# Joined load of k and q, earlier output weights, and weight conversion on GpSimd in an attention and gated-MLP kernel

## The chip, the core and the metric

The kernel runs on one NeuronCore of a Trainium2 chip. The metric is the device time of one execution in microseconds (us), taken as the median of several executions of the same program. Five engines work side by side, each through its own queue in order: TensorE (PE, matmuls; PEld are its weight loads), VectorE (DVE), ScalarE (ACT), GpSimd (POOL) and SyncE (SP), which here issues every DMA.

## What is computed

For 8 batches of 8 heads, 576 positions and head dimension 64, the kernel does causal attention with a bias made of prefix sums, and puts the result through a gated MLP with a spatial mixing step.

```python
scores = scale * np.matmul(q, k.transpose(0, 1, 3, 2))
cum = np.cumsum(np.maximum(s, 0.0), axis=-1)
bias = -(cum[:, :, :, None] - cum[:, :, None, :])
scores = np.where(causal, -1000000000.0, scores + np.minimum(bias, 0.0))
attn = softmax(scores)
x = np.matmul(attn, v)                       # (B, S, 512) after joining heads
h = np.maximum(x @ w_in, 0.0)                # d_ff 1024
u, v = h[..., :512], h[..., 512:]
v_n = (v - mu) / np.sqrt(var + 1e-06)
v_s = np.einsum('ts,bsd->btd', w_spatial, v_n) + b_spatial[None, :, None]
out = (u * v_s) @ w_out
```

q, k, v and s are float32, and the MLP's weights w_in, w_spatial and w_out come as they are drawn: w_in and w_out are 64-bit floats.

## The kernel before

Matmuls run in 16 bits. Every float32 operand is split into a high part (its float16 rounding) and a low part (the rest, in float16), and a product is three matmuls: high by high, high by low, low by high.

**Heads in pairs.** The 64 heads are 32 pairs, four pairs to a batch. For a pair, `load_raw` fetches k and q as float32 tiles with the head dimension in the partitions, both into partitions 64 to 127 and again into 0 to 63 (four loads for pairs 3 to 5; three for later pairs, where the second load of q is left out). `split_raw` makes four float16 tiles, each one of three that rotate: KA and QA hold the high parts in partitions 64 to 127 (and constants and prefix sums in the lower ones, `aux_rows`), KB and QB hold low and high parts stacked, so that one matmul over 128 partitions adds both cross products. k goes through VectorE (L251 rounds, L255 subtracts), q through ScalarE (L259) and GpSimd (L239, four pieces of 288 columns). For pairs below 6 the copies of the high parts to the other half of the partitions are ScalarE steps (L249, L261); for later pairs they are DMAs from SBUF to SBUF (L257, L263). Pairs 0 to 2 multiply the float32 tiles directly (L310). The raw tiles of k and q have one buffer each.

**Attention.** `s_pass` makes a pair's scores (L316) in PSUM, masks and takes the minimum (VectorE, L320), takes the exponential (ScalarE, L326), normalises into high and low parts (L335, L336), and transposes the result by DMA (L341). `av_pass` multiplies by V (L414, L421) and evacuates the result to xt: high part on ScalarE (L427), low part on VectorE (L428). The bank of av has one buffer.

**MLP.** `mlp` runs by batch: the gate half (L455) with its normalisation (L471 to L489), the other half (L505), the spatial product (L518 to L521) with the gating (L523 to L526), and the output product (L540), evacuated at L543 and stored at L545.

**Weights.** The 64-bit weights are fetched as integers (`fetch_w64`), and `split_w64` makes float32 of them by bit operations on VectorE (L167, L168, L170), zeroes what is too small (ScalarE squares at L173, VectorE compares and multiplies at L174), and hands the float32 tile to `split_w`: high part on ScalarE (L148); low part on VectorE (L150), or by a scaling on ScalarE (L152) and a subtraction on GpSimd (L153). The constants `N_W1`, `N_W2`, `N_W3` and `N_W4` are 2, 1, 5 and 0: two tiles of w_in's gate half, one of its other half and all five of w_spatial take VectorE; three and two tiles of w_in and the four of w_out take GpSimd. `load_wout` fetches and converts one of four tiles of w_out, all through the one buffer of the tag "wst", which also holds one tile of w_in before and the bias rows.

**Order.** Every step is put into a list with a position (`at`, `units`); the list is sorted by position and emitted in that order. TensorE runs exactly in the order of emission. On the other engines a scheduler that simulates the program orders instructions, with what is emitted earlier ahead of what is emitted later. Up to position 12.416 (`G_END`) most steps are also kept behind the last step that is marked as first on their engine. Pair p's scores lie at positions 2p to 2p + 5/3, its av at 2p + 3.72 (pair 3: 9.4), and batch b's MLP at 8b + 10.3 to 8b + 18; the output product of batch 0 begins at 16.1. The load of pair p lies at 2p - 5.2, its split at 2p - 1.2. `load_wsp` lies at 11 to 12.2, `load_wtail` at 13.

Of the kernel before, what the change touches and what calls it, by code (L numbers as in the profile page):

```python
# [7 lines left out]
F16 = mybir.dt.float16  # L8
# [10 lines left out]
SW = 64.0  # L19
# [10 lines left out]
@with_exitstack  # L30
def attn_gated_mlp(ctx, tc, qT, kT, v, s, w_in, w_spT, b_sp, w_out, outT):
    nc = tc.nc
    P = 128
    NHB, D, H, S = qT.shape
    B, H = NHB // 2, 2 * H
    NPAIR = H // 2
# [76 lines left out]
    def native_tiles(pair):  # L113


        hs = slice(2 * (pair % 2), 2 * (pair % 2) + 2)
        tags = (("g1", "g2"), ("xt1", "xt2"), ("xt1", "xt2"), ("rawk", "rawq"))[pair]
        raw_tiles(pair // 2, hs, tags, (1, 2, 2, N_RB)[pair])
        first_ins["c"] = [raw_rows(pair // 2, hs, nm, 1) for nm in "kq"][1].ins

# [26 lines left out]
    def split_w(dst1, dst2, raw, sc, dve):  # L147
        nc.scalar.activation(dst1, raw, AF.Copy, bias=0.0, scale=sc)  # L148
        if dve:
            nc.vector.scalar_tensor_tensor(out=dst2, in0=raw, scalar=sc, in1=dst1, op0=ALU.mult, op1=ALU.subtract)  # L150
            return
        nc.scalar.activation(raw, raw, AF.Copy, bias=0.0, scale=sc)  # L152
        nc.gpsimd.tensor_tensor(out=dst2, in0=raw, in1=dst1, op=ALU.subtract)  # L153

# [5 lines left out]

    def split_w64(dst1, dst2, st, tag_t, dve):

# [10 lines left out]
        nc.scalar.activation(sq, sq, AF.Square, bias=0.0, scale=1.0)  # L173
        nc.vector.scalar_tensor_tensor(out=tf, in0=sq, scalar=2.0 ** -30, in1=tf, op0=ALU.is_ge, op1=ALU.mult)  # L174
        split_w(dst1, dst2, tf, SW, dve)

# [6 lines left out]
    def load_win(hf, c):  # L183
        split_w64(win1[:, c, hf * NF:(hf + 1) * NF], win2[:, c, hf * NF:(hf + 1) * NF], wsts.pop((hf, c)),
                  "hv" if hf else "ob", c < (N_W1 if hf else N_W2))

    def load_wout(c):
        split_w64(wo1[:, c], wo2[:, c], fetch_w64(w_out[c * P:c * P + P], "wst"), "ob", c < N_W4)

    def load_wsp(c):  # L190
        st = wk.tile([P, S], F32, tag="ob", bufs=2, name="wsp_st")
        nc.sync.dma_start(out=st, in_=w_spT[c * P:c * P + P])
        split_w(ws1[:, c], ws2[:, c], st, SWSP, c < N_W3)

    def load_wtail():
        s4 = wk.tile([P, S], F32, tag="ob", bufs=2, name="wsx_st")
        nc.sync.dma_start(out=s4[0:TAIL], in_=w_spT[NFULL * P:S])
        nc.sync.dma_start(out=s4[TAIL:2 * TAIL], in_=w_spT[NFULL * P:S])
        split_w(wx1, wx2, s4, SWSP, N_W3 > 4)
        bf = wk.tile([1, S], F32, tag="ob", bufs=2, name="bf")  # L200
# [16 lines left out]

    def raw_tiles(hb, hs, tags=("rawk", "rawq"), bufs=1):

        for tag, nm in zip(tags, "kq"):  # L220
            raws[hb, hs.start, nm] = wk.tile([P, hs.stop - hs.start, S], F32, tag=tag, bufs=bufs, name=f"{nm}raw{hb}")

    def raw_rows(hb, hs, nm, top):
        rows = slice(64 * top, 64 * top + 64)
        if nm == "k" or top or 2 * hb + hs.start // 2 < N_CD:
            return nc.sync.dma_start(out=raws[hb, hs.start, nm][rows], in_=(kT if nm == "k" else qT)[hb, :, hs])

    def load_raw(hb, pr):
        hs = slice(2 * pr, 2 * pr + 2)
        raw_tiles(hb, hs, bufs=N_RB)  # L230
        for top in (1, 0):
            for nm in "kq":
                raw_rows(hb, hs, nm, top)

    def pieces(eng, out, in0, in1):
        for j in range(2):
            for hf in range(2):
                c = slice(hf * TH, hf * TH + TH)
                eng.tensor_tensor(out=out[:, j, c], in0=in0[:, j, c], in1=in1[:, j, c], op=ALU.subtract)  # L239

    def split_raw(hb, nm, pr):

        p = 2 * hb + pr
        i = p % 3
        raw = raws[hb, 2 * pr, nm]
        lo, hi = slice(0, 64), slice(64, 128)
        if nm == "k":
            if p < N_CD:
                nc.scalar.copy(KA[i][hi], raw[hi])  # L249
            if p < N_KA:  # L250
                nc.vector.tensor_copy(KB[i], raw)  # L251
            else:
                nc.scalar.copy(KB[i], raw)
            eng = nc.gpsimd if p < N_KP else nc.vector
            eng.tensor_tensor(out=KB[i][lo], in0=raw[lo], in1=KB[i][lo], op=ALU.subtract)  # L255
            if p >= N_CD:
                nc.sync.dma_start(out=KA[i][hi], in_=KB[i][hi])  # L257
        else:
            (nc.scalar.copy if p < N_QA else nc.vector.tensor_copy)(QA[i][hi], raw[hi])  # L259
            if p < N_CD:  # L260
                (nc.scalar.copy if p < N_QA else nc.vector.tensor_copy)(QB[i][lo], raw[lo])  # L261
            else:
                nc.sync.dma_start(out=QB[i][lo], in_=QA[i][hi])  # L263
            pieces(nc.gpsimd, QB[i][hi], raw[hi], QA[i][hi])

# [125 lines left out]
    def av_pass(pair):  # L391
# [40 lines left out]
    def mlp(b):  # L432
# [32 lines left out]
        for t in range(NC5):  # L465
# [13 lines left out]
            nc.vector.bn_aggr(out=mv, in_=st if tail else st[:, 0])  # L479
            nc.gpsimd.tensor_scalar(rs, mv[:, 1:2], 1.0e-6, None, op0=ALU.add)  # L480
            nc.gpsimd.tensor_tensor(out=rs, in0=rs, in1=mhalf, op=ALU.pow)
# [4 lines left out]
            else:  # L486
                d1, d2 = vn1[:, t], vn2[:, t]
            nc.scalar.activation(d1, hv, AF.Copy, bias=0.0, scale=SVN)
            nc.vector.scalar_tensor_tensor(out=d2, in0=hv, scalar=SVN, in1=d1, op0=ALU.mult, op1=ALU.subtract)  # L489
            if tail:  # L490
# [91 lines left out]
    at(-18.9, True, native_cum, 1)  # L582
    at(0.5, True, behind, "c", load_raw, 1, 1)
    at(0.6, True, init_static, 0)
# [12 lines left out]
    for hb in range(2, NHB):  # L597
        for pr in range(2):
            p = 2 * hb + pr
            at(2 * p - 5.2, False, load_raw, hb, pr)  # L600
            at(2 * p - 1.2, False, aux_rows, p)
            for nm in "kq":
                at(2 * p - 1.2, False, split_raw, hb, nm, pr)
        at(4 * hb - 0.5, False, fetch_v, hb)
        at(4 * hb + 1.5, False, load_v, hb)
    for c in range(KC):
# [4 lines left out]
        at(11 + 0.4 * c, False, load_wsp, c)  # L611
        at(13.5 + 0.5 * c, False, load_wout, c)
    at(13, False, load_wtail)
    for p in range(NP):
        units([2 * p + k / 3 for k in range(6)], p < 4, s_pass, p)
        at_av = 2 * p + 3.72 if p != 3 else 9.4
        units([at_av], p < 4, av_pass, p)
    for b in range(B):
# [61 lines left out]
```

## Time and profile before

| | |
|---|---|
| three runs | 740.40, 741.07, 741.52 us |
| median | 741.07 us |
| profiled execution | 741.57 us |
| its span in the trace | 739.8 us |
| mean granted clock of TensorE | 0.928 |
| DMA traffic | 119.09 MB, 161 GB/s |
| HBM read, written | 46.71 MB, 9.44 MB |

The span is what the trace covers of the profiled execution; 1.8 us lie around it. In the rows of the profile, "L414" is line 414 of the kernel, a name such as `xt<-av` is what is written and read, "x32" a count, and an arrow in brackets names the time an engine stood idle before the instruction and what ended that idle time. In a row of the waits the numbers are the total in us, how often, and the longest. In a row of the timeline the first number is the start in us and the second the length. A group of instructions has, behind its count, busy us, mean ns of one, and the idle time before.

### The profile page before, as it was taken

The numbers are of one execution on the slowest core, as the hardware profiler recorded it, in microseconds if no ns is written. First come the engines' busy times: TensorE is split into PE (matmuls) and PEld (weight loads), VectorE is DVE, ScalarE is ACT, GpSimd is POOL, SyncE is SP. The second block draws the span as 40 slices with busy tenths as digits, with TensorE's granted clock in tenths as the row PEclk, the third lists the DMA queues.
The fourth block names the chain that finished last, engine by engine and source line by source line (L and its number), as shares of the span: only waits on it lengthen the run. The fifth ranks groups of instructions, "written<-read, shape, count | busy, mean of one in ns | idle before, by whom it ended". The sixth has DMA issues, their size and how long they took to land. (4 is left out here: it accounts for less than half of the span.)

```text
span 739.8 us, 15952 instructions
## 1 busy us (share of the span) xinstructions
PE 609.2 (82%) x5696; PEld 420.0 (57%) x5696; DVE 607.5 (82%) x1660; ACT 528.2 (71%) x1334; POOL 175.8 (24%) x226
## 2 busy tenths in 40 slices
PE   4555454576659899999899899899998998999998
PEld 2243222255436677667665667477756774677676
DVE  8968699969839999889988997899979997985431
ACT  5957677567638788879786978778787887875422
POOL 7002335303302322142213321132223222100100
PEclk9777677599759999999999999999999999999999
DMA  9798776948638779987998799969997798465001
GB/s 203 177 223 166 187 179 155 205 110 195 159 85 190 150 152 189 208 193 127 202 209 196 139 202 187 216 132 193 190 216 145 180 184 161 76 126 121 33 13 64
DMA packets 243261, 119.09 MB, mean 161 GB/s; under 512 B 213887, under 2 KB 227373, under 8 KB 243182
## 3 DMA queue, kind: packets, MB, share of 16 engines
q1 hardware_dynamic: 243182, 118.08, 75.1%
q8 instruction: 44, 0.72, 0.4%
q14 instruction: 35, 0.29, 0.1%
HBM read 46.71 MB, written 9.44 MB: 76 GB/s over the span
## 5 line engine op out<-in xcount | busy, mean ns | idle before, releaser
L239 POOL TENSOR_TENSOR QB<-qraw,QA 64x288 f16<-64x288 f32 x116 | 123.4, 1095 | 296.5 <-ACT QA L259 219.8
L320 DVE CUSTOM_DVE_ANT_0 psS<-psS,mb 128x512 f32<-128x512 f32 (+2 forms) x320 | 155.0, 495 | 14.9 <-PE psS L316 13.9
L326 ACT ACTIVATE p<-psS,mx 128x256 f32<-128x256 f32 (+3 forms) x256 | 132.9, 523 | 48.0 <-DVE mx L320 44.2
L336 DVE SCALAR_TENSOR_TENSOR pb<-p,sm,pb 128x384 f16<-128x384 f32 (+3 forms) x256 | 129.7, 548 | 0.5 <-ACT pb L335 0.3
L335 ACT ACTIVATE pb<-p,sm 128x384 f16<-128x384 f32 (+3 forms) x256 | 122.7, 556 | 9.1 <-ACT p L326 5.1
L540 PE MATMUL ops<-g,wo 128*128 128x288 f16 x768 | 105.3, 291 | 16.7 <-ACT wo L148 12.0
L316 PE MATMUL psS<-KA,QA 128*128 128x128 f16 (+1 forms) x348 | 82.2, 310 | 44.3 <-ACT p L326 32.8
L505 PE MATMUL ups<-xt,win 128*128 128x288 f16 x768 | 105.1, 290 | 15.7 <-ACT win L148 6.0
L518 PE MATMUL sps<-ws,vn 128*128 128x288 f16 x768 | 105.7, 288 | 11.0 <-DVE g L523 11.0
L455 PE MATMUL vps<-win,xt 128*128 128x512 f16 (+1 forms) x576 | 106.1, 356 | 10.5 <-ACT ob L543 8.5
L505 PEld LDWEIGHTS <-win 128*128 128x128 f16 x768 | 74.7, 99 | 45.0 <-issue 12.4
L540 PEld LDWEIGHTS <-wo 128*128 128x128 f16 x768 | 75.4, 99 | 42.9 <-ACT wo L148 12.6
L518 PEld LDWEIGHTS <-vn 128*128 128x128 f16 x768 | 74.3, 98 | 36.4 <-issue 14.1
L316 PE MATMUL psS<-KB,QB 128*128 128x128 f16 (+1 forms) x348 | 88.9, 306 | 0.0
L455 PEld LDWEIGHTS <-xt 128*128 128x128 f16 (+1 forms) x576 | 48.9, 104 | 60.3 <-issue 22.1
L414 PE MATMUL av<-pT,V 128*64 128x128 f16 (+2 forms) x960 | 67.8, 295 | 13.8 <-DMA pT<-pb 13.8
L414 PEld LDWEIGHTS <-V 128*64 128x64 f16 x960 | 55.1, 119 | 31.6 <-issue 20.0
L316 PEld LDWEIGHTS <-QA 128*128 128x128 f16 x348 | 30.3, 102 | 45.4 <-issue 37.7
L480 POOL TENSOR_SCALAR rs<-mv 128x1 f32<-128x1 f32 x40 | 10.3, 257 | 190.3 <-DVE mv L479 173.7
L326 ACT ACTIVATION_READ_ACCUMULATOR p<-psS,mx 128x1 f32 x256 | 50.6, 198 | 0.0
L543 ACT ACTIVATE ob<-ops 128x288 f32<-128x288 f32 x64 | 25.0, 413 | 30.9 <-PE ops L540 17.4
L316 PEld LDWEIGHTS <-QB 128*128 128x128 f16 x348 | 29.9, 103 | 26.5 <-issue 19.7
(117 smaller groups left out, 890.3 us busy)
## 6 DMA issues: line engine op xcount, KB each, us to landing
kraw<-in_kT_dram SPq DMA_DIRECT2D x61, 288.0 KB
qraw<-in_qT_dram SPq DMA_DIRECT2D x35, 288.0 KB
out_dram<-ob SPq DMA_DIRECT2D x32, 288.0 KB
vraw<-in_v_dram SPq DMA_DIRECT2D x16, 512.0 KB
wst<-in_w_in_dram SPq DMA_DIRECT2D x8, 512.0 KB
QB<-QA SPq DMA_DIRECT2D x26, 144.0 KB
KA<-KB SPq DMA_DIRECT2D x26, 144.0 KB
vraw<-in_v_dram SPq DMA_DIRECT2D x16, 128.0 KB
```

Source lines behind the costliest of these rows:

```text
L239: eng.tensor_tensor(out=out[:, j, c], in0=in0[:, j, c], in1=in1[:, j, c], op=ALU.subtract)
L316: nc.tensor.matmul(ps[m, c0:c0 + w], U[i][:, g, q0:q0 + n], T[i][:, g, k0:k0 + w], start=st, stop=not st)
L320: nc.vector.tensor_tensor_reduce(out=ps[:, c0:c0 + w], in0=ps[:, c0:c0 + w], in1=mask, op0=ALU.add, op1=ALU.min, scale=-0.125, scalar=3.0e ...
L326: nc.scalar.activation(p32, ps[:, c0:c0 + w], AF.Exp, bias=mx[:, col:col + 1], scale=-1.0, accum_out=sm[:, acc:acc + 1])
L335: nc.scalar.activation(dst[:, off:off + w], p32, AF.Copy, bias=0.0, scale=sm[:, col:col + 1])
L336: nc.vector.scalar_tensor_tensor(out=dst[:, n + off:n + off + w], in0=p32, scalar=sm[:, col:col + 1], in1=dst[:, off:off + w], op0=ALU.mul ...
L414: nc.tensor.matmul(dst, V[i][:, jc, h + j], rhs, start=jc == n == 0 and q0 > 0, stop=jc == 3 and n == 2)
L455: nc.tensor.matmul(ps[m, 0:w], xx[:, c, t * P:t * P + (m.stop - m.start)], ww[:, c, NF + g * w:NF + g * w + w], start=c == n == 0, stop=c ...
L505: nc.tensor.matmul(ps[:, 0:TH], ww[:, c, fs], xx[:, c, ts], start=n == 0, stop=n == 3 * KC - 1)
L518: nc.tensor.matmul(ps[:, 0:TH], vv[:, c, fs], ww[:, c, ts], start=n == 0, stop=False)
L540: nc.tensor.matmul(ps[:, 0:TH], ww[:, f, ms], gg[:, f, ts], start=n == 0, stop=n == 3 * FC - 1)
L543: nc.scalar.activation(ob[:, ts], ps[:, 0:TH], AF.Copy, bias=0.0, scale=1.0 / (SG * SW))
```

## The change

One input, kqT, holds k's and q's transposed rows one above the other, so that a pair's k and q come by one load of 128 partitions: k in the lower 64, q in the upper. The raw tile has two buffers. VectorE rounds k into a tile kh in the lower partitions, two DMAs copy that into KA and KB, and a third copies QA's high part into QB; this holds for all pairs from 3 on. `split_w64` now compares and scales on GpSimd, multiplies on GpSimd in two halves, and subtracts there in two halves, for all twelve tiles. The low parts of w_spatial are subtracted on GpSimd too, in two halves, after a scaling on ScalarE. The evacuation of av becomes a unit of its own, 0.35 positions behind its matmuls. The factor 64 of the normalised gate goes into the reciprocal root. `load_wout` of tile c moves from position 13.5 + 0.5 c to 10.6 + 1.1 c.

```diff
@@ split_w
         nc.scalar.activation(raw, raw, AF.Copy, bias=0.0, scale=sc)
-        nc.gpsimd.tensor_tensor(out=dst2, in0=raw, in1=dst1, op=ALU.subtract)
+        h = raw.shape[1] // 2
+        for c in (slice(0, h), slice(h, 2 * h)):
+            nc.gpsimd.tensor_tensor(out=dst2[:, c], in0=raw[:, c], in1=dst1[:, c], op=ALU.subtract)
@@ split_w64
         nc.scalar.activation(sq, sq, AF.Square, bias=0.0, scale=1.0)
-        nc.vector.scalar_tensor_tensor(out=tf, in0=sq, scalar=2.0 ** -30, in1=tf, op0=ALU.is_ge, op1=ALU.mult)
-        split_w(dst1, dst2, tf, SW, dve)
+        nc.gpsimd.tensor_scalar(sq, sq, 2.0 ** -30, SW, op0=ALU.is_ge, op1=ALU.mult)
+        h = n // 2
+        for c in (slice(0, h), slice(h, n)):
+            nc.gpsimd.tensor_tensor(out=tf[:, c], in0=sq[:, c], in1=tf[:, c], op=ALU.mult)
+        nc.scalar.copy(dst1, tf)
+        for c in (slice(0, h), slice(h, n)):
+            nc.gpsimd.tensor_tensor(out=dst2[:, c], in0=tf[:, c], in1=dst1[:, c], op=ALU.subtract)
@@ load_wsp, load_wtail
-        split_w(ws1[:, c], ws2[:, c], st, SWSP, c < N_W3)
+        split_w(ws1[:, c], ws2[:, c], st, SWSP, False)
...
-        split_w(wx1, wx2, s4, SWSP, N_W3 > 4)
+        split_w(wx1, wx2, s4, SWSP, False)
@@ load_raw, split_raw
+    def load_raw(p):
+
+        hb, pr = divmod(p, 2)
+        raws[p] = wk.tile([P, 2, S], F32, tag="raw", bufs=2, name=f"raw{p}")
+        nc.sync.dma_start(out=raws[p], in_=kqT[hb, :, 2 * pr:2 * pr + 2])
...
         if nm == "k":
...
+            kh = wk.tile([64, 2, S], F16, tag="kh", bufs=1, name=f"kh{p}")
+            nc.vector.tensor_copy(kh, raw[lo])
+            nc.sync.dma_start(out=KA[i][hi], in_=kh)
+            nc.sync.dma_start(out=KB[i][hi], in_=kh)
+            nc.vector.tensor_tensor(out=KB[i][lo], in0=raw[lo], in1=kh, op=ALU.subtract)
         else:
...
+            nc.scalar.copy(QA[i][hi], raw[hi])
+            nc.sync.dma_start(out=QB[i][lo], in_=QA[i][hi])
+            for j in range(2):
+                for c in (slice(0, TH), slice(TH, S)):
+                    nc.gpsimd.tensor_tensor(out=QB[i][hi, j, c], in0=raw[hi, j, c], in1=QA[i][hi, j, c],
+                                            op=ALU.subtract)
@@ av_pass
+        yield
         both = [(av, x1[:, pr, 0:512], x2[:, pr, 0:512])]
@@ mlp
-            nc.gpsimd.tensor_scalar(rs, mv[:, 1:2], 1.0e-6, None, op0=ALU.add)
+
+            nc.gpsimd.tensor_scalar(rs, mv[:, 1:2], 1.0e-6, 1.0 / (SVN * SVN), op0=ALU.add, op1=ALU.mult)
...
-            nc.scalar.activation(d1, hv, AF.Copy, bias=0.0, scale=SVN)
-            nc.vector.scalar_tensor_tensor(out=d2, in0=hv, scalar=SVN, in1=d1, op0=ALU.mult, op1=ALU.subtract)
+            nc.scalar.copy(d1, hv)
+            nc.vector.tensor_tensor(out=d2, in0=hv, in1=d1, op=ALU.subtract)
@@ the plan
-        at(13.5 + 0.5 * c, False, load_wout, c)
+        at(10.6 + 1.1 * c, False, load_wout, c)
...
-        units([at_av], p < 4, av_pass, p)
+        units([at_av, at_av + 0.35], p < 4, av_pass, p)
@@ kernel
-        'qT': inputs['q'].reshape(2 * B, H // 2, S, D).transpose(0, 3, 1, 2),
-        'kT': inputs['k'].reshape(2 * B, H // 2, S, D).transpose(0, 3, 1, 2),
+        'kqT': _np.concatenate([inputs[n].reshape(2 * B, H // 2, S, D).transpose(0, 3, 1, 2) for n in 'kq'], axis=1),
```

More of the change, by code (lines that the diff above doesn't have):

```diff
@@ L30, in attn_gated_mlp @@
 @with_exitstack
-def attn_gated_mlp(ctx, tc, qT, kT, v, s, w_in, w_spT, b_sp, w_out, outT):
+def attn_gated_mlp(ctx, tc, kqT, v, s, w_in, w_spT, b_sp, w_out, outT):
     nc = tc.nc
     P = 128
-    NHB, D, H, S = qT.shape
-    B, H = NHB // 2, 2 * H
+    NHB, D, H, S = kqT.shape
+    B, H, D = NHB // 2, 2 * H, D // 2
     NPAIR = H // 2
@@ L116, in native_tiles @@
         hs = slice(2 * (pair % 2), 2 * (pair % 2) + 2)
-        tags = (("g1", "g2"), ("xt1", "xt2"), ("xt1", "xt2"), ("rawk", "rawq"))[pair]
-        raw_tiles(pair // 2, hs, tags, (1, 2, 2, N_RB)[pair])
-        first_ins["c"] = [raw_rows(pair // 2, hs, nm, 1) for nm in "kq"][1].ins
+        tags = ((("g1", 1), ("g2", 1)), (("xt1", 2), ("xt2", 2)), (("xt1", 2), ("xt2", 2)))[pair]
+        raw_tiles(pair // 2, hs, tags)
+        first_ins["c"] = [raw_rows(pair // 2, hs, nm) for nm in "kq"][1].ins
     def native_sel(pair):
@@ L159, in fetch_w64, with split_w64 @@
         return st
-    def split_w64(dst1, dst2, st, tag_t, dve):
+    def split_w64(dst1, dst2, st, tag_t):
         n = st.shape[1]
@@ L184, in load_win @@
         split_w64(win1[:, c, hf * NF:(hf + 1) * NF], win2[:, c, hf * NF:(hf + 1) * NF], wsts.pop((hf, c)),
-                  "hv" if hf else "ob", c < (N_W1 if hf else N_W2))
+                  "hv" if hf else "ob")
     def load_wout(c):
-        split_w64(wo1[:, c], wo2[:, c], fetch_w64(w_out[c * P:c * P + P], "wst"), "ob", c < N_W4)
+        split_w64(wo1[:, c], wo2[:, c], fetch_w64(w_out[c * P:c * P + P], "wst"), "ob")
     def load_wsp(c):
@@ L216, in attn_gated_mlp @@
     raws = {}
[L218 to L243, printed above, removed]
+    def raw_tiles(hb, hs, tags):
+        for (tag, bufs), nm in zip(tags, "kq"):
+            raws[hb, hs.start, nm] = wk.tile([P, 2, S], F32, tag=tag, bufs=bufs, name=f"{nm}raw{hb}")
+    def raw_rows(hb, hs, nm):
+        src = kqT[hb, 0:64, hs] if nm == "k" else kqT[hb, 64:128, hs]
+        return nc.sync.dma_start(out=raws[hb, hs.start, nm][64:128], in_=src)
@@ L244, in split_raw @@
+    def load_raw(p):
+        hb, pr = divmod(p, 2)
+        raws[p] = wk.tile([P, 2, S], F32, tag="raw", bufs=2, name=f"raw{p}")
+        nc.sync.dma_start(out=raws[p], in_=kqT[hb, :, 2 * pr:2 * pr + 2])
+    def split_raw(nm, p):
         i = p % 3
-        raw = raws[hb, 2 * pr, nm]
+        raw = raws[p] if nm == "k" else raws.pop(p)
         lo, hi = slice(0, 64), slice(64, 128)
         if nm == "k":
[L248 to L257, printed above, removed]
-        else:
[L259 to L264, printed above, removed]
@@ L582, in attn_gated_mlp @@
     at(-18.9, True, native_cum, 1)
-    at(0.5, True, behind, "c", load_raw, 1, 1)
+    at(0.5, True, behind, "c", load_raw, 3)
     at(0.6, True, init_static, 0)
@@ L588, in attn_gated_mlp @@
     for nm in "kq":
-        at(2.1, True, split_raw, 1, nm, 1)
+        at(2.1, True, split_raw, nm, 3)
     at(2.1, True, native_tiles, 2)
@@ L599, in attn_gated_mlp @@
             p = 2 * hb + pr
-            at(2 * p - 5.2, False, load_raw, hb, pr)
+            at(2 * p - 5.2, False, load_raw, p)
             at(2 * p - 1.2, False, aux_rows, p)
             for nm in "kq":
-                at(2 * p - 1.2, False, split_raw, hb, nm, pr)
+                at(2 * p - 1.2, False, split_raw, nm, p)
         at(4 * hb - 0.5, False, fetch_v, hb)
```

## The prediction

> **What bounds the kernel now.** I read the busy totals first, then busy time by stage, then what TensorE waited for in each stage, then the timelines around its longest waits.
>
> ```profile
> PE 609.2 (82%) x5696; PEld 420.0 (57%) x5696; DVE 607.5 (82%) x1660; ACT 528.2 (71%) x1334; POOL 175.8 (24%) x226
> ```
>
> TensorE and VectorE are equally busy over the whole, which hides two stages. The rows below give start:end, length, then busy time (and count) of PE, PEld, DVE, ACT, POOL, then granted clock, DMA share and GB/s.
>
> ```profile
> 0.00:213.24 213.24, 114.47 (x908) 71.38 (x909) 176.89 (x439) 142.46 (x332) 62.24 (x72) 0.78 0.77 174
> 213.24:672.00 458.76, 430.69 (x4254) 301.59 (x4253) 408.42 (x1172) 362.78 (x950) 109.29 (x144) 0.99 0.83 171
> ```
>
> From 213 us on PE is busy 430.69 of 458.76 us at clock 0.99: it is the bound, and 28 us is all that better order could give there. Before 213 it is idle 213.24 - 114.47 = 98.8 us. VectorE works 177 of those 213 us, so it is the busiest, but it also has pauses. What PE waited for, first in that stage, then (last row) after it:
>
> ```profile
> PE psS L316 <- ACT p L326: 30.4, 6, 9.7
> PE av L414 <- DMA pT<-pb: 13.0, 3, 7.4
> PE ops L540 <- ACT wo L148: 12.0, 2, 7.8
> PE psS L316 <- DMA KA<-cc: 9.6, 1, 9.6
> ...
> PE ops L540 <- POOL wo L153: 3.8, 2, 2.5
> ...
> PE vps L455 <- ACT ob L543: 8.5, 5, 2.4
> ```
>
> So the change must be priced in the first 213 us. What it saves there moves the start of the saturated stage and reaches the end nearly whole. The steady stage I leave unpriced, at 0, with 8 us (the size of its largest wait) either way for a changed order.
>
> **The change, part by part.** The base is the profiled execution, 741.57 us (span 739.8 and 1.8 around it); the runs' median is 741.07, 0.5 lower.
>
> *A. The evacuation of av is emitted 0.35 positions later.*
>
> ```profile
> 53.96 3.15 PE L414 MATMUL av<-pT,V 128*64 128x384 f16 x27 [7.44 <-DMA pT<-pb]
> ...
> 57.36 0.60 ACT L427 ACTIVATE xt<-av 128x512 f16<-128x512 f32 x1 [7.67 <-PE av L414]
> ...
> 58.19 0.69 ACT L326 ACTIVATE q<-psS,mx 128x512 f32<-128x512 f32 x1
> ...
> 58.86 1.92 ACT L335 ACTIVATE pb<-p,sm 128x384 f16<-128x384 f32 x4
> ```
>
> PE waits 7.44 us for the transposed weights; ScalarE has the evacuation at the head of its queue and stands 7.67 us behind it, though the softmax work of 0.69 and 1.92 us behind it needs no av. Emitted later, that work should go first: at least 2.6 us, at most the 7.67. I take 2.6, since little more was ready. Later on the evacuation also comes later; cost 0, hidden by the one-pair distance to the next av, and if that cover fails, see the third rival.
>
> *B. Joined load, copies by DMA.*
>
> ```profile
> kraw<-in_kT_dram SPq DMA_DIRECT2D x61, 288.0 KB
> qraw<-in_qT_dram SPq DMA_DIRECT2D x35, 288.0 KB
> ...
> QB<-QA SPq DMA_DIRECT2D x26, 144.0 KB
> KA<-KB SPq DMA_DIRECT2D x26, 144.0 KB
> ```
>
> Three pairs stay as 6 loads of 288 KB; 29 pairs take one load of 576 KB and three copies of 144 KB. That is 1,728 + 16,704 + 12,528 = 30,960 KB in place of 96 x 288 + 52 x 144 = 35,136: 4.2 MB less. For pairs 3 to 5 four loads become one: 576 KB less each, 3.3 us at the stage's 174 GB/s. In SP's queue a pair goes from five issues to four (pairs 3 to 5: four both ways). The new wait is that KA, KB and the low half of QB hang on DMAs behind SP's queue, where transposes, aux rows and loads are queued; for pairs 3 to 5 ScalarE wrote them directly. In exchange ScalarE is freed of these:
>
> ```profile
> 67.02 1.15 ACT L249 CAST KA<-kraw 64x1152 f16<-64x1152 f32 x1
> ...
> 69.25 1.15 ACT L261 CAST QB<-qraw 64x1152 f16<-64x1152 f32 x1
> 70.30 0.68 ACT L326 ACTIVATE p<-psS,mx 128x512 f32<-128x512 f32 x1
> ...
> 71.13 0.64 PE L316 MATMUL psS<-KA,QA 128*64 128x512 f16 x2 [7.04 <-ACT p L326]
> ```
>
> The exponential at 70.30, for which PE waits 7.04 us, stands behind 2.3 us of copies that go. VectorE's two steps on k remain.
>
> *C. The raw tile gets two buffers.*
>
> ```profile
> 69.30 7.69 POOL L239 TENSOR_TENSOR QB<-qraw,QA 64x288 f16<-64x288 f32 x4 [51.13 <-ACT QA L259]
> ...
> 77.02 0.47 SPq L226 DMA_DIRECT2D qraw<-in_qT_dram  x1
> ...
> 79.93 1.21 SPq L214 DMA_DIRECT2D KA<-cc  x2
> ...
> 85.39 0.27 PE L316 MATMUL psS<-KA,QA 128*128 128x128 f16 x1 [9.55 <-DMA KA<-cc]
> ```
>
> The next pair's load waits for POOL to finish with the single buffer (69.30 + 7.69 = 76.99), and the aux rows behind it leave SP only by 81.1, which PE feels as 9.55 us. With a second buffer the aux rows can go earlier, but PE still needs POOL's pieces (76.99) and the new copies; the ends are 0 and 85.39 - 76.99 = 8.4, and I take half, 4.
>
> A to C together: 2.6 + 2.3 + 4 = 9; the bytes I leave out, as they shorten a transfer that the same waits already count. Each saving exposes the next limit (DMA share is 0.77 in this stage), so I count 6, with ends 0 and 18 (7.67 + 2.3 + 8.4).
>
> *D. Lo parts of the weights and the conversion's last step go from VectorE to GpSimd.*
>
> ```profile
> L174 DVE SCALAR_TENSOR_TENSOR wt<-wst,wt 128x512 f32<-128x512 f32 x12 | 9.6, 806 | 0.0
> L153 POOL TENSOR_TENSOR win<-wt,win 128x512 f16<-128x512 f32 x5 | 5.9, 1192 | 10.8 <-ACT wt L152 10.8
> L152 ACT ACTIVATE wt<-wt 128x512 f32<-128x512 f32 x9 | 5.6, 623 | 0.1
> ...
> L150 DVE SCALAR_TENSOR_TENSOR ws<-wsp_st,ws 128x576 f16<-128x576 f32 x4 | 3.0, 751 | 2.0 <-ACT ws L148 1.9
> ...
> L150 DVE SCALAR_TENSOR_TENSOR win<-wt,win 128x512 f16<-128x512 f32 x3 | 2.1, 687 | 0.2 <-ACT win L148 0.2
> ```
>
> VectorE loses 9.6 + 3.0 + 2.1 and one wx step of ws' size, 0.75: 15.4 us. ScalarE loses 5.6 and gains five scalings of about 0.7. GpSimd gains per 64-bit tile one whole-tile step and four half pieces; the trace has no such piece.
>
> ```profile
> L239 POOL TENSOR_TENSOR QB<-qraw,QA x116: 727/876/4127, 13.7 to 615.6; 64x288 f16<-64x288 f32 x116
> ...
> L153 POOL TENSOR_TENSOR wo<-wt,wo 128x512 f16<-128x512 f32 x4 | 4.6, 1156 | 27.0 <-ACT wt L152 27.0
> ```
>
> A half piece of 256 lies between half of 1.16 (512 wide) and the whole of it; I take 0.73, the fastest of the 288-wide pieces, and 1.0 for the whole-tile step with its single input. That makes 12 x (1.0 + 4 x 0.73) = 47 us, and 10 x 0.73 = 7 for ws and wx, less the nine old steps, 5.9 + 4.6: GpSimd works 44 us more in a stage where it has 62 of 213. Its time is free, but it holds up VectorE:
>
> ```profile
> 191.60 4.05 POOL L239 TENSOR_TENSOR QB<-qraw,QA 64x288 f16<-64x288 f32 x4 [3.19 <-issue]
> ...
> 193.85 1.21 DVE L170 SCALAR_TENSOR_TENSOR wt<-wst,wt 128x512 uint32<-128x512 uint32 x1
> ...
> L170 DVE SCALAR_TENSOR_TENSOR wt<-wst,wt x12: 676/677/1214, 33.4 to 207.0; 128x512 uint32<-128x512 uint32 x12
> ```
>
> While four pieces ran (4.05 us) the L170 step took 1.21 where 0.677 is its median, 0.53 more. If VectorE is held so two to three times in four pieces (an estimate), that is 1.1 to 1.6 us per 4.05, say 0.35 per us of GpSimd. 44 x 0.35 = 15 us given back against 15.4 removed: I take D at 0. Its ends: no hold-up, -15.4 times VectorE's busy share 177/213 = 0.83, so -13; hold-up for the whole of each GpSimd instruction, 44 x 0.83 - 15.4 = +21.
>
> The Trainium skill ("SBUF — State Buffer", section "SBUF: two separate sides") says that a VectorE instruction with two SBUF inputs and a GpSimd instruction that reads SBUF exclude each other for the whole instruction of the one that came first. The lengthened step above agrees in kind; its 0.53 is less than a whole piece of 0.73. By that page the sum of D would lie at the +21 end if GpSimd always came first.
>
> The layer-norm fold (64 into the reciprocal root) replaces a VectorE step of two tensors and a constant by one of the same two tensors, and a scaled copy on ScalarE by a plain one. No row shows the new forms at this size; the tensors read and written are the same, and so I take 0.
>
> *E. Output weights from position 10.6 to 13.9 in place of 13.5 to 15.*
>
> ```profile
> 162.84 0.38 SPq L158 DMA_DIRECT2D wst<-in_w_out_dram  x1
> ...
> 199.42 0.52 SPq L158 DMA_DIRECT2D wst<-in_w_out_dram  x1
> ...
> 205.35 0.43 DVE L167 TENSOR_SCALAR wt<-wst 128x512 uint32<-128x512 uint32 x1 [2.21 <-DMA wst<-in_w_out_dram]
> ...
> 211.08 0.66 PE L540 MATMUL ops<-g,wo 128*128 128x288 f16 x2 [7.77 <-ACT wo L148]
> ```
>
> Four tiles pass one buffer, the first fetched at 162.8, the last at 199.4: one per 12.2 us. The last lands at about 205.3, is converted, and PE goes on at 211.08; the waits on wo are 12.0 + 3.8 = 15.8 us. Begun earlier by 13.5 - 10.6 = 2.9 positions, the last by 1.1. The stage's position 13.5 lies near 163 us, so a position is some 12 us and the last tile comes about 13 us sooner. What moves is each tile's fetch and its VectorE, ScalarE and GpSimd steps, and behind them in the shared staging buffers the w_spatial tiles. VectorE's three steps a tile that stay (0.68 for L170, and two like it at most: 4 x 2 = 8 us) leave the stall, where VectorE was idle, and go where it is full. So of 15.8 I count 13 gone and 5 given back: 8. Ends 0 (the one buffer, now shared in this order with the bias rows, keeps the last tile late) and 15.8.
>
> **Sum:** 6 + 0 + 8 = 14; 741.6 - 14 = 727.6, less the 0.5 by which the median stands below: **727 us**.
>
> **Rivals.**
> *1. GpSimd holds VectorE* (slower). Place: about 33 us (the first of the L170 steps) to 213 us, where VectorE is busiest. Price: D at +21, less 14, so +7: 748. It decides from D = +14, that is when 44 us of GpSimd hold VectorE for (14 + 15.4)/44 = 0.67 of their time. For: the L170 row. Against: that row gives about half of this, and the halves are short. The page named above is the rule for it. Chance 0.1.
> *2. The weights come no earlier* (the change doesn't do what it says). One buffer, and fetches behind transposes in SP's queue: E = 0, 735. For: the 12.2 us spacing is set by buffer and queue, not by position. Against: before 162.8 us none of the four was fetched at all. Chance 0.15.
> *3. The later evacuation costs in the steady stage.* PE's next gate matmuls need xt, and the softmax now goes ahead of it. 28 us of PE idle there would grow by the 2.6 us of A's work per batch, seven times: +18, so 745 with the rest as forecast. For: VectorE is busy 408 of 459 us. Against: PE has output matmuls to do between. Chance 0.1.
> *4. VectorE gets its time and the steady order improves too.* D at -13, 8 us more in the steady stage or A to C in full: 706 to 714. For: the first stage has 98.8 us of idle PE. Against: the hold-ups. Chance 0.15.
>
> **How the numbers follow.** Forecast 0.5 (719 to 734). Range: with rivals 2 and 4 down to 710, and up to where rival 3 begins, **710 to 744**. A measurement of this kernel tells about 0.2% (1.5 us) from no change. Faster: 0.5 + 0.15 + 0.15, and a little of rival 3: 0.82. Same: 0.05, from the edges of rivals 2 and 3. Slower: 0.13.
>
> **What would show it.** A right: no ScalarE wait of 7 us on av near 57 us. B and C right: PE's 9.55 us wait on the aux rows shrinks below 5, and 7.04 below 5. D right: VectorE's busy time is within 5 us of 607.5 although 15.4 us of work left it, with two-input steps lengthened beside GpSimd's pieces. E right: waits of L540 on wo under 4 us in place of 15.8, and PE's saturated stage beginning about 14 us sooner. Wrong: a new wait of PE on w_spatial's tiles or on the DMA copies KA, KB, QB; steady PE idle far from 28 us; GpSimd's added time far from 44 us.

## The result, and the profile after

The changed kernel is **slower**, by 1.3%: 750.54 us (median of 4 runs, 748.96 to 752.89) against 741.3 (4 runs), a ratio of 1.0128, 95% interval 1.0105 to 1.0150. 727 was forecast. The profiled execution took 751.11 us, with a span of 749.3.

The busy totals of TensorE and VectorE look as the prediction had them, and say nothing of where the loss is. GpSimd's don't: it works 247.6 us in place of 175.8, 72 more, where 44 were forecast.

```profile
PE 605.9 (81%) x5696; PEld 418.6 (56%) x5696; DVE 605.1 (81%) x1640; ACT 520.1 (69%) x1324; POOL 247.6 (33%) x287
```

The stages say where it is. The border lies at the first gate matmul (the product of L455) of batch 1, where the first stage's stalls are over, and the second stage ends at that of the last batch. These are the rows of busy time by stage (start:end, length, PE, PEld, DVE, ACT, POOL, clock, DMA share, GB/s), first of the kernel before:

```profile
0.00:231.20 231.20, 132.43 (x1077) 84.18 (x1078) 187.68 (x471) 154.25 (x363) 66.09 (x76) 0.79 0.74 168
231.20:686.90 455.70, 427.43 (x4247) 300.33 (x4245) 403.13 (x1154) 358.05 (x938) 105.45 (x141) 0.99 0.84 172
```

then of the kernel after:

```profile
0.00:228.70 228.70, 128.29 (x1076) 82.43 (x1077) 186.88 (x447) 144.19 (x350) 133.93 (x136) 0.78 0.70 166
228.70:696.60 467.90, 428.31 (x4247) 300.69 (x4245) 401.54 (x1157) 360.18 (x941) 109.66 (x142) 0.98 0.74 160
```

The first stage is only 2.5 us shorter, where 14 was forecast. The steady stage, which was left at 0 with 8 us either way, is 467.9 - 455.7 = **12.2 us longer** at nearly the same PE work. Together with an end that is 0.2 us shorter, these make up the 9.5 us between the two spans. So there are two questions: what ate the first stage's gain, and what PE lost in a stage where it is the bound.

**The steady stage.** PE's idle time in it grows from 28.3 to 39.6 us. These are its main waits there (total us, times, longest), of the kernel before:

```profile
PE vps L455 <- ACT ob L543: 8.5, 5, 2.4
PE sps L518 <- DVE g L523: 6.1, 10, 0.7
PE ups L505 <- ACT u L508: 5.8, 5, 1.4
PE psS L316 <- ACT p L326: 2.4, 8, 0.3
```

and of the kernel after, all of them but 0.2 us:

```profile
PE sps L514 <- DVE g L519: 14.6, 7, 3.1
PE psS L310 <- ACT p L320: 14.2, 12, 2.4
PE vps L450 <- ACT ob L539: 10.4, 6, 2.2
```

The wait for VectorE's gating step g grows by 8.5 us and the one for ScalarE's exponential p by 11.8, while the 5.8 on u go. To see what holds VectorE up, here are its groups in the stage (line, operation, out<-in, count | busy, mean ns | idle before, and for what), two of the kernel before and their counterparts after:

```profile
L251 DVE CAST KB<-kraw 128x1152 f16<-128x1152 f32 x20 | 17.4, 870 | 0.0
L482 DVE TENSOR_SCALAR hv<-hv,mv,rs 128x512 f32<-128x512 f32 (+1 forms) x30 | 17.2, 572 | 12.6 <-POOL rs L481 12.5
```

```profile
L248 DVE CAST kh<-raw 64x1152 f16<-64x1152 f32 x20 | 16.7, 834 | 18.3 <-DMA KB<-kh 18.3
L478 DVE TENSOR_SCALAR hv<-hv,mv,rs 128x512 f32<-128x512 f32 (+1 forms) x30 | 16.3, 545 | 6.5 <-POOL rs L477 6.5
```

The cast of k cost VectorE no wait before; now it stands 18.3 us in all for the copies out of kh, which has one buffer. Another wait shrinks by 6.0. These are the two largest changes in a VectorE idle time that grows by 13.8 us in all, from 52.6 to 66.4. How much of this reaches PE, sums of waits can't tell. One place where it does, in the timeline of the kernel after (start, length, engine):

```profile
331.40 0.89 DVE L248 CAST kh<-raw 64x1152 f16<-64x1152 f32 x1 [0.23 <-DMA KB<-kh]
...
348.22 2.83 SPq L221 DMA_DIRECT2D KA<-cc  x3
...
351.74 0.53 SPq L250 DMA_DIRECT2D KB<-kh  x1
...
354.37 0.75 DVE L248 CAST kh<-raw 64x1152 f16<-64x1152 f32 x1 [2.74 <-DMA KB<-kh]
355.04 1.48 DVE L274 SCALAR_TENSOR_TENSOR V<-vraw,V 128x1280 f16<-128x1280 f32 x1
356.44 0.44 DVE L519 SCALAR_TENSOR_TENSOR g<-sps,u 128x288 f32<-128x288 f32 x1
...
356.94 1.26 PE L514 MATMUL sps<-ws,vn 128*128 128x288 f16 x9 [3.06 <-DVE g L519]
```

One pair's cast is done at 332.3, but its second copy is issued only at 351.74, behind transposes and the aux rows in SP's queue, and the buffer is free some 2.6 us later. So kh is held 22 us for a transfer of 2.6, and the steady stage's other pairs look alike: 14.6 to 19.4 us from a cast to the issue of its copy. The cast of the next pair, which nobody needs yet, stands at the head of VectorE's queue for it; the gating step at 356.44, which frees the PSUM bank that PE needs, is queued behind it and a step on V, and PE waits 3.06 us. This happens once in each of five batches: VectorE stands 2.1 to 2.7 us at the cast, and PE waits 2.4 to 3.1 right after, 13.5 of the 14.6 us on g. The longer waits on the exponential lie elsewhere in the batch, and the trace doesn't tie them to a cast.

**The first stage.** What PE waited for up to 250 us in the kernel after (total us, times, longest):

```profile
PE psS L310 <- ACT p L320: 15.9, 6, 8.9
PE av L408 <- DMA pT<-pb: 15.6, 3, 8.8
PE vps L450 <- ACT win L180: 11.7, 2, 11.1
PE sps L517 <- DMA wx<-bp: 9.1, 1, 9.1
PE sps L514 <- POOL ws L155: 8.1, 1, 8.1
...
PE vps L450 <- POOL win L182: 6.0, 2, 5.0
PE psS L310 <- DMA KA<-kh: 4.5, 1, 4.5
PE sps L516 <- ACT wx L148: 4.4, 1, 4.4
```

Much of what was to go did go: the wait on the exponential falls from 30.4 to 15.9 us, the 9.6 on the aux rows is a wait of 4.5 on a copy of kh, and the 15.8 us on the output weights are gone. In their place stand 9.1 + 8.1 + 4.4 = 21.6 us on the spatial weights and the bias rows, which share staging buffers with the output weights (before: none), and 11.7 + 6.0 = 17.7 us on w_in's gate half (before: 9.1 us, on w_in's other half). PE's idle time in the stage is 100.4 us, against 98.8 before. The waits on w_in hang on GpSimd (kernel after, its groups, then its busy row from 76 to 108 us, in which POOL is the fifth engine):

```profile
L176 POOL TENSOR_SCALAR wst<-wst 128x512 f32<-128x512 f32 x12 | 26.6, 2213 | 28.5 <-ACT wst L175 27.8
L179 POOL TENSOR_TENSOR wt<-wst,wt 128x256 f32<-128x256 f32 x24 | 22.7, 968 | 0.6
L182 POOL TENSOR_TENSOR win<-wt,win 128x256 f16<-128x256 f32 x16 | 11.9, 766 | 5.9 <-ACT win L180 5.8
```

```profile
76.00:108.00 32.00, 13.63 (x107) 6.40 (x108) 22.66 (x49) 15.02 (x32) 29.49 (x27) 0.63 0.63 169
```

GpSimd is busy 29.5 of those 32 us, and VectorE has 9.3 us to spare.

### The profile page after: what moved, and what is told of

Its sections match the earlier page's. It is cut to its first block, busy times and chain, and to the rows that moved or that the text cites. A ratio compares the mean times of both kernels' runs of the same rounds, so it can differ in the third digit from the quotient of the medians.

```text
span 749.3 us, 15946 instructions
## 1 busy us (share of the span) xinstructions
PE 605.9 (81%) x5696; PEld 418.6 (56%) x5696; DVE 605.1 (81%) x1640; ACT 520.1 (69%) x1324; POOL 247.6 (33%) x287
## 2 busy tenths in 40 slices
DMA packets 243037, 114.81 MB, mean 153 GB/s; under 512 B 213471, under 2 KB 226957, under 8 KB 242958
## 5 line engine op out<-in xcount | busy, mean ns | idle before, releaser
L257 POOL TENSOR_TENSOR QB<-raw,QA 64x288 f16<-64x288 f32 x116 | 124.6, 1105 | 250.9 <-ACT QA L253 213.0
L320 ACT ACTIVATE p<-psS,mx 128x128 f32<-128x128 f32 (+3 forms) x256 | 132.9, 524 | 66.5 <-DVE mx L314 56.3
L330 DVE SCALAR_TENSOR_TENSOR pb<-p,sm,pb 128x384 f16<-128x384 f32 (+3 forms) x256 | 136.6, 567 | 3.9 <-ACT pb L329 3.6
L450 PE MATMUL vps<-win,xt 128*128 128x512 f16 (+1 forms) x576 | 107.6, 359 | 28.5 <-ACT win L180 11.7
L514 PE MATMUL sps<-ws,vn 128*128 128x288 f16 x768 | 109.9, 295 | 22.7 <-DVE g L519 14.6
L514 PEld LDWEIGHTS <-vn 128*128 128x128 f16 x768 | 75.9, 100 | 49.3 <-issue 16.6
L536 PE MATMUL ops<-g,wo 128*128 128x288 f16 x768 | 101.7, 286 | 0.2 <-DVE g L522 0.2
L501 PEld LDWEIGHTS <-win 128*128 128x128 f16 x768 | 74.5, 98 | 34.8 <-issue 12.2
L408 PE MATMUL av<-pT,V 128*64 128x128 f16 (+2 forms) x960 | 66.1, 291 | 15.7 <-DMA pT<-pb 15.6
L408 PEld LDWEIGHTS <-V 128*64 128x64 f16 x960 | 53.4, 118 | 34.2 <-issue 21.4
L521 ACT CAST g<-g 128x288 f16<-128x288 f32 x64 | 27.1, 429 | 48.2 <-DVE g L519 47.2
L310 PEld LDWEIGHTS <-QA 128*128 128x128 f16 x348 | 30.4, 103 | 42.5 <-issue 30.7
L314 DVE DVE_READ_ACCUMULATOR2_ANT mx<- 128x1 f32 x320 | 44.0, 138 | 0.0
```

Of the source, the lines that this page charges most:

```text
L257: nc.gpsimd.tensor_tensor(out=QB[i][hi, j, c], in0=raw[hi, j, c], in1=QA[i][hi, j, c], op=ALU.subtract)
L310: nc.tensor.matmul(ps[m, c0:c0 + w], U[i][:, g, q0:q0 + n], T[i][:, g, k0:k0 + w], start=st, stop=not st)
L314: nc.vector.tensor_tensor_reduce(out=ps[:, c0:c0 + w], in0=ps[:, c0:c0 + w], in1=mask, op0=ALU.add, op1=ALU.min, scale=-0.125, scalar=3.0e ...
L320: nc.scalar.activation(p32, ps[:, c0:c0 + w], AF.Exp, bias=mx[:, col:col + 1], scale=-1.0, accum_out=sm[:, acc:acc + 1])
L330: nc.vector.scalar_tensor_tensor(out=dst[:, n + off:n + off + w], in0=p32, scalar=sm[:, col:col + 1], in1=dst[:, off:off + w], op0=ALU.mul ...
L408: nc.tensor.matmul(dst, V[i][:, jc, h + j], rhs, start=jc == n == 0 and q0 > 0, stop=jc == 3 and n == 2)
```

## The experiments

Three theories were set against each other: theory 1, VectorE's cast into kh stands for the copies; theory 2, the later evacuation costs; theory 3, the conversion on GpSimd costs. Each ratio is to runs of the kernel before on the same chip (its medians were 740.9 to 742.5); the experiments ran on several chips. "First" is the start of batch 1's gate matmuls, "steady" the time from there to those of the last batch, each from one profiled execution. That execution lies within 3 us of the median, but for e1 (771.9 us, 8 above) and e6 (749.5 us, 5 above), whose stages may be too long by a part of that.

| kernel | us | ratio, 95% interval | first | steady |
|---|---|---|---|---|
| before | 741.3 | 1 | 231.2 | 455.7 |
| after | 750.5 | 1.0128, 1.0105 to 1.0150 | 228.7 | 467.9 |
| e1 second kh | 763.8 | 1.0313, 1.0256 to 1.0370 | 232.2 | 485.2 |
| e2 output weights late | 762.2 | 1.0273, 1.0249 to 1.0297 | 239.8 | 467.3 |
| e3 old conversion | 743.4 | 1.0017, 0.9992 to 1.0042 | 217.9 | 467.7 |
| e4 evacuation back | 756.8 | 1.0211, 1.0167 to 1.0255 | 232.9 | 468.1 |
| e5 late cast | 764.0 | 1.0297, 1.0272 to 1.0322 | 226.7 | 481.9 |
| e6 old loads | 744.8 | 1.0040, 1.0021 to 1.0058 | 235.8 | 458.9 |
| e7 old loads, old conversion | 744.2 | 1.0027, 1.0007 to 1.0048 | 231.1 | 456.9 |
| e8 late cast, old conversion | 753.7 | 1.0157, 1.0121 to 1.0192 | 218.2 | 479.7 |
| e9 joined load alone | 746.6 | 1.0064, 1.0045 to 1.0084 | 225.2 | 468.1 |
| e10 joined up to pair 7, old conversion | **730.4** | 0.9834, 0.9793 to 0.9875 | 220.9 | 455.8 |
| e11 both casts late | 757.9 | 1.0216, 1.0175 to 1.0257 | 229.8 | 472.5 |
| e12 cast one pair back | 748.3 | 1.0097, 1.0061 to 1.0134 | 232.8 | 462.1 |
| e13 both casts back, old conversion | 735.4 | 0.9906, 0.9873 to 0.9940 | 220.9 | 458.6 |
| e14 joined up to pair 7, new conversion | 741.2 | 1.0002, 0.9978 to 1.0026 | 227.0 | 459.8 |

**e1: another buffer for kh.** The second buffer takes no more SBUF: from pair 10 on every other pair uses the staging buffer that the weights no longer need.

```diff
-            kh = wk.tile([64, 2, S], F16, tag="kh", bufs=1, name=f"kh{p}")
+            kh = wk.tile([64, 2, S], F16, tag="kh" if p < 10 or p % 2 else "wst", bufs=1, name=f"kh{p}")
```

> The changed kernel, but from pair 10 on the rounded k alternates between its own buffer and the staging buffer that the weights no longer need, so that a cast need not wait for the copies of the pair before. Theory 1 (the one buffer of kh holds VectorE up: 15.4 us of waits in the five batches from 290 to 682 us): the waits of the cast go below 2 us, batches last 77 us in place of 79.3, and the kernel takes 739 to 743 us. Theory 2 (the later evacuation of av costs in the steady stage) and theory 3 (GpSimd's conversion): 749 to 752 us, as the changed kernel's 750.5, and PE waits on VectorE and ScalarE as before.

A miss: 763.8. VectorE's wait moved and grew (waits of VectorE in e1):

```profile
DVE kh L248 <- DMA raw<-in_kqT_dram: 25.0, 15, 3.4
```

With kh free, the scheduler put the cast still earlier, and there it stands for the load of its raw tile. The buffer was not the whole of it: the cast waits for a DMA either way.

**e2: output weights back.** `at(13.5 + 0.5 * c, ...)` for `load_wout`, the rest as after.

> The changed kernel with the output weights back at positions 13.5 to 15. If they displace the spatial weights through the shared staging buffers (21.6 us of PE waits on ws, wx and the bias rows), these waits shrink below 5 us and the waits on the output weights return with 10 to 16 us: the end within 4 us of 750.5. If the earlier position were a pure gain of 8 us, as forecast, this takes 758 us. If it cost more than it brought, 740 to 745 us.

It took 762.2, near the 758 of a gain: batch 1's gate comes 239.8 - 228.7 = 11.1 us later. The waits on the spatial weights and bias rows fall from 21.6 to 5.3 us, so the earlier output weights do displace them. But PE waits 27.7 us on the output weights (row below, e2), more than the 15.8 of before; each tile's compare and multiplies are GpSimd's now, ahead of the step at L180.

```profile
PE ops L536 <- ACT wo L180: 27.7, 3, 12.0
```

**e3: old conversion.** `split_w`, `split_w64` and their callers as before.

> The changed kernel with the old conversion: last step on VectorE, low parts on VectorE or in one piece on GpSimd. Theory 3 (GpSimd's conversion costs: PE waits 17.7 us on converted w_in between 77 and 107 us, GpSimd busy 19.6 of 20 us there): those waits go below 6 us, the first stage ends some 8 us sooner, 742 to 746 us; batches still take 79.3 us. Theories 1 and 2: within 3 us of 750.5, as the loss lies in the steady stage.

As theory 3 has it for the first stage, 10.8 us shorter; the steady stage stays at 467.7, as theories 1 and 2 have it. Both losses exist, and apart. The median is 7.2 us below the changed kernel's (this profiled execution was 2.7 us faster than e3's median). In the same 32 us as above, GpSimd is busy 13 us and VectorE 29.4 (e3):

```profile
76.00:108.00 32.00, 16.31 (x109) 7.03 (x109) 29.38 (x59) 21.72 (x43) 12.98 (x11) 0.71 0.76 182
```

**e4: evacuation back** in one unit with its matmuls (no `yield`, no second position).

> The changed kernel with av evacuated in the same unit as its matmuls, as before. Theory 2: batches back at 77 us, 740 to 743 us. Theories 1 and 3: batches stay at 79 us, 749 to 753 us, and the wait of PE near 55 to 70 us grows by up to 3 us.

Steady 468.1: the later evacuation costs nothing there, so theory 2 falls. In the first stage it gains 232.9 - 228.7 = 4.2 us, and 756.8 us in all is more than any theory had. The gain isn't where part A put it. There, near 50 us, PE waits 3.16 us on the transposed weights in e4 and 3.62 in the kernel after; what e4 has more are waits on w_in's other half (10.5 us, from 135 us on; none after) and on the bias rows (14.9 us; 9.1 after).

**e5 and e8: the cast kept back by two pairs** (e8 with the old conversion too).

```diff
-            nc.vector.tensor_copy(kh, raw[lo])
+            cast = nc.vector.tensor_copy(kh, raw[lo]).ins
+            if p >= 8:
+                tc.add_manual_dep(cast, last_dve[p - 2].name, nosync, reason="late")
```

Here `last_dve[p]` is the last VectorE step of pair p's softmax.

> The changed kernel with one more order: from pair 8 on the cast of k into kh stays behind the last VectorE step of the softmax two pairs earlier, so that it isn't moved up to the moment the copies of the pair before are due. Theory 1 (VectorE stands in its queue at the cast for a DMA that lands later than the order supposed): waits of the cast below 3 us in place of 19.4, batches 77 us in place of 79.3, 739 to 744 us. Rival (the steady loss comes from something else in the new order, and the cast's waits are only where it shows): waits of the cast go, but batches stay at 79 us or more, 748 us and up.

> The changed kernel with the late cast and with the old conversion. Theory 1 with the conversion's price of 10.7 us in the first stage: first stage ends near 218 us as in the run with the old conversion, batches 77 us, 727 to 733 us. Rival as for the late cast alone: near 740 us.

Both missed. The cast no longer waits, but now ScalarE's cast of q waits for the load of its raw tile, whose buffers come free later; PE waits for the last rows of the normalised gate, vx (waits of e5):

```profile
ACT QA L255 <- DMA raw<-in_kqT_dram: 24.0, 13, 3.9
...
PE sps L519 <- DMA vx<-tl: 13.3, 5, 3.0
```

**e6 and e7: old loads and splits** (e7 with the old conversion, so that only the output weights, the evacuation and the folded factor are left of the change).

> The changed kernel with the loads and splits of k and q as before: four or three loads, ScalarE's copies for pairs below 6, one raw buffer; the rest stays changed. Theory 1: the whole steady loss is in this part, batches 77 us; the first stage as after or up to 5 us worse; 739 to 746 us. Rival (evacuation, layer norm or chance of order): batches stay at 79 us, 748 us and up.

> The kernel before with only three edits: earlier output weights, later evacuation of av, factor folded into the root. If the loss lies in the joined load (steady) and in GpSimd's conversion (start), this keeps the gains of about 11 us (weights) and 4 us (evacuation) without either: 727 to 733 us, faster than before. If gains and losses don't add up so: 738 us or more.

Steady is back at 458.9 and 456.9: the loss there is in the joined load and its copies, in the kernel with each conversion. The two kernels differ by the conversion alone and by 0.6 us in their medians: with the old loads it costs next to nothing. But e7 missed in total. Without the joined load, earlier weights and later evacuation bring the first stage nothing (231.1 against 231.2); PE's waits moved from the output weights to the tail of the spatial ones (e7, first stage), 12.8 + 11.9 = 24.7 us in place of 15.8:

```profile
PE sps L522 <- ACT wx L148: 12.8, 1, 12.8
PE sps L523 <- DMA wx<-bp: 11.9, 1, 11.9
```

Nor does the later evacuation do what part A says. In e7, with it, ScalarE still stands behind av near 57 us, as it did before (7.67):

```profile
58.65 0.60 ACT L428 ACTIVATE xt<-av 128x512 f16<-128x512 f32 x1 [7.03 <-PE av L414]
```

**e9: the joined load alone**, in the kernel before.

> The kernel before with the joined load alone: one load, two raw buffers, kh and three DMA copies; output weights, evacuation, conversion and layer norm as before. If the joined load gains in the first stage (the runs with old loads begin batch 1's gate 7 to 13 us later than those with the joined load) and costs in the steady one: batch 1's gate before 228 us, 465 to 470 us from there to the gate of the last batch in place of 455.7, in all 741 to 752 us. If the loss belongs to the other edits: 458 us there and 730 to 736 us in all.

As expected if it does both: 6.0 us gained in the first stage, 12.4 lost in the steady one, 746.6 in all. It shortens PE's waits of 7.04 and 9.55 us on the exponential and the aux rows to 2.60 and, on the copy KA<-kh, 5.45. It also shortens ScalarE's wait behind av, with the evacuation where it was (e9):

```profile
51.73 0.60 ACT L414 ACTIVATE xt<-av 128x512 f16<-128x512 f32 x1 [1.13 <-PE av L401]
```

Its cast waits as after (the row is VectorE's group in e9):

```profile
L241 DVE CAST kh<-raw 64x1152 f16<-64x1152 f32 x29 | 24.3, 836 | 19.9 <-DMA KB<-kh 19.8
```

**e10: joined up to pair 7, old conversion.** From pair 8 on, two raw tiles and the old split:

```diff
+        raws[p] = [wk.tile([P, 2, S], F32, tag="raw", bufs=2, name=f"{nm}raw{p}") for nm in "kq"]
+        nc.sync.dma_start(out=raws[p][0][64:128], in_=kqT[hb, 0:64, hs])
+        nc.sync.dma_start(out=raws[p][1][64:128], in_=kqT[hb, 64:128, hs])
+        nc.sync.dma_start(out=raws[p][0][0:64], in_=kqT[hb, 0:64, hs])
...
+            nc.vector.tensor_copy(KB[i], raw)
+            nc.vector.tensor_tensor(out=KB[i][lo], in0=raw[lo], in1=KB[i][lo], op=ALU.subtract)
+            nc.sync.dma_start(out=KA[i][hi], in_=KB[i][hi])
```

> The changed kernel with the old conversion, and with the joined load for pairs 3 to 7 only; from pair 8 on two raw tiles of one buffer's size each take the place of the joined one, loaded and cast as in the kernel before, with no kh. If the joined load's gain lies in the first stage and its cost in the steady one, and they can be had apart: batch 1's gate near 218 us, 457 us from there to the last, 726 to 733 us in all. If the gain and the loss hang together (the order chosen by the scheduler decides): 738 us or more.

730.4 us, faster than both kernels. Its stages are the first of the joined load and the steady one of before:

```profile
0.00:220.90 220.90, 130.60 (x1077) 82.09 (x1078) 187.44 (x465) 145.06 (x351) 78.19 (x74) 0.80 0.75 172
220.90:676.70 455.80, 424.59 (x4246) 299.52 (x4244) 403.98 (x1160) 360.66 (x944) 105.51 (x143) 1.00 0.83 172
```

**e11: both casts two pairs back**, q's on ScalarE too, by the same kind of dependency.

> The changed kernel with both casts kept back: kh's on VectorE and QA's on ScalarE stay behind the softmax of the pair two earlier on their engine. If the loss is an engine standing at a cast for a DMA (kh's copies in the changed kernel, the raw load in the kernel with one late cast, where ScalarE waited 24 us on it): both waits below 4 us and 455 to 460 us of steady stage, 736 to 743 us in all. If the order of the rest costs, as the wait on vx's DMA of 13.3 us in the kernel with one late cast: 468 us or more, 750 us and up.

The second outcome: 472.5. Neither cast waits long any more, but the cast now lies beside the end of the layer norm, and PE waits for vx (timeline of PE, e11):

```profile
350.35 0.40 PE L522 MATMUL sps<-wx,vx 128*128 128x288 f16 x1 [3.24 <-DMA vx<-tl]
```

**e12 and e13: the casts three pairs back** (`last_dve[p - 3]`), where the free slot of KB had put the cast in the kernel before; e12 moves VectorE's cast alone, e13 both, with the old conversion.

> The changed kernel with the cast into kh kept behind the softmax of the pair three earlier (the place that the free KB slot gave the cast in the kernel before), so one pair earlier than in the kernels with late casts, and still some 15 us behind the copies of the pair before. If the steady loss is the cast standing for kh's copies, and the late casts lost only because they lay beside the layer norm's tail: waits of the cast below 3 us, no wait on vx's DMA, 455 to 459 us from batch 1's gate to the last one's, 737 to 742 us in all. If the joined load loses through something else: 466 us or more, 748 us and up.

> As the run before, with QA's cast kept back in the same way and the old conversion. First theory: batch 1's gate near 218 us, 455 to 459 us of steady stage, 726 to 731 us in all, level with the kernel that joins the load up to pair 7. Else: 466 us or more of steady stage, 737 us and up.

In e12 the wait is gone, without a new one on vx (VectorE's group; in e13 PE waits 4.4 us on vx):

```profile
L248 DVE CAST kh<-raw 64x1152 f16<-64x1152 f32 x29 | 22.1, 763 | 0.0
```

The steady stage is 462.1 in e12 and 458.6 in e13: between the two outcomes. 5.8 (against the changed kernel) and 9.1 (against e3) of the 12.2 us come back in place of all, while the first stage gets 4.1 and 3.0 us longer. And what comes back isn't PE's wait on the gating step: that is 12.4 us in e12 and 15.9 in e13, against 14.6 and, in e3, 12.1. In e12 the subtraction of k (1.35 us) now stands ahead of that step. What shrinks is PE's wait on ScalarE's output step ob (10.4 us after; none in e12, 1.9 in e13), and in e13 the one on the exponential (6.7, against 15.3 in e3; 17.7 in e12). e13 is the only kernel with the joined load throughout that beats the kernel before.

**e14: joined up to pair 7, new conversion.**

> The joined load for pairs 3 to 7 only, with GpSimd's conversion as in the change. If the conversion's price and the steady loss are independent: batch 1's gate near 229 us (8 to 11 us behind the same kernel with the old conversion), steady stage 456 to 458 us, 738 to 742 us. If the conversion costs less once the steady loss is gone: 730 to 735 us.

741.2 against e10's 730.4: the conversion on GpSimd costs some 11 us also without the steady loss. By the stages 6.1 of it lie in the first and 4.0 in the steady one.

## Why the prediction was wrong

**The steady stage, "unpriced, at 0".** This is the step that decided the sign; the 12.2 us are more than even the 8 it allowed. Part B named the readers of the copies KA, KB and QB as the ones that wait, and not the writer: kh has one buffer, so the next cast must wait for the copies to land, and VectorE's queue stands behind it. That the joined load with its copies is where the 12 us go is shown: 467 to 468 us in all five kernels that have it without a moved cast or a second kh (after, e2, e3, e4, e9), 455.7 to 459.8 in the five that haven't it from pair 8 on (before, e6, e7, e10, e14). That the cast's wait is the means is not shown. In the trace of the kernel after it stands right before five of PE's long waits; but where it is gone (e12, e13), half to three quarters of the loss come back while PE's wait on the gating step stays. In e1, e5, e8 and e11 the scheduler's new order made other waits as large. It may be that the place of k's two steps among VectorE's others costs, with the wait as one part of it; that is argued and not tested, and the cause of the rest stays open. The third rival had the right stage and the wrong place, the evacuation (e4).

**D, taken at 0: it cost 7 to 11 us** wherever the joined load is in (medians: 7.2 by e3, 10.3 by e8 against e5, 10.8 by e14 against e10), and 0.6 with the old loads (e6 against e7). VectorE's sum was right: 15.4 us of work left it and it is busy 186.9 us in the first stage against 187.7, so 14.6 came back, where 15 was forecast, as longer steps (the softmax's low parts 620 ns in place of 557, the third bit step of the weights 911 in place of 768). What failed is "its time is free". No run had shown the 1.0 us of the whole-tile step; it took 2.2. The half pieces of the 64-bit tiles, sized at 0.73, took 0.77 to 0.97. So the weights' steps on GpSimd grew by 65.8 us and not 44, it filled up between 76 and 108 us, and the converted weights came late; the chain through GpSimd was never priced as a path. The first rival looked for the loss in VectorE being held up beside GpSimd's steps. The rule of the Trainium skill ("SBUF — State Buffer", section "SBUF: two separate sides") points to that too. The trace agrees in so far as those 14.6 us came back. But the loss was in GpSimd's own queue, beside which VectorE had 9.3 of 32 us to spare.

**E, 8 us: 11.1** by e2 in the changed kernel, but A and E together brought nothing in the kernel with the old loads (e7). The waits on the spatial weights, which the prediction listed only as "what moves", took the place of those on w_out.

**A, 2.6 us: 4.2** by e4, but not by its mechanism, so that the likeness is luck. With the evacuation moved and the old loads, ScalarE still stands 7.03 us behind av (e7); with the joined load and the evacuation in place it stands 1.13 (e9). The wait that A was to remove went with the joined load.

**B and C**, 4 of the 6 us counted for A to C: the joined load alone brings 6.0 in the first stage (e9), and 7.1 to 13.2 beside the other edits (e6 against after; e7 against e3). Here the mechanism held: both waits that were named shrank, and the DMA traffic fell by 4.3 MB (119.09 to 114.81), as counted. (576 KB at 174 GB/s are 3.4 us and not 3.3; the sum doesn't use them.) But the parts don't add: what one edit gains in the first stage depends on which wait is next.

**The folded factor, 0**: VectorE's step took 0.672 in place of 0.678 us in the steady stage.

**The signs that the prediction set.** All four signs of being right came at the places named, but for the end of E's: ScalarE's longest wait on av is 3.4 us in the first stage, the two waits of PE are 2.81 and 4.48, VectorE's busy time is 605.1, and the waits on w_out are gone; the saturated stage began 2.5 us sooner in place of 14. All three signs of being wrong came too: new waits on the spatial weights (21.6 us) and on a copy (4.5), 39.6 us of idle PE in the steady stage in place of 28, and GpSimd's added time.

## What to carry to other kernels

When a step gets an intermediate tile of one buffer that a DMA reads, the writer of the next one waits for that DMA, its time in the issuing queue included, and all that is queued behind the writer on its engine waits too; ask what sets a step's place in an in-order queue, a matmul that is long done or a transfer that has just been issued. Work moved to an idle engine is a path with its own length, not a free sum: price its longest stretch where the consumer waits. A wait that goes away after an edit isn't yet the edit's work: see whether it goes without it too (A and e9). An edit that helps while DMA and engines fill up can cost where one engine is saturated, and can be limited to the stage in which it helps (e10: 730.4 us).

## What the hardware showed that was not expected

GpSimd's compare-and-scale of a 128x512 float32 tile, one input read at every second element, took 1.98 to 2.97 us in its twelve cases (median 2.04), longer than its subtraction of two tiles of that size in the kernel before (1.16). And the 144 KB copy from SBUF to SBUF took 2.6 us from its issue until its source buffer was free in the place shown; in the steady stage the next cast began 2.5 to 3.6 us after the issue.
